# Retention and squared-ReLU FFN: a third room for one block's activations, and a reordered start

## The chip, the core and the metric

The kernel runs on one core of a Trainium2 chip. A core has five engines that run side by side: TensorE (PE, matmuls), VectorE (DVE), ScalarE (ACT), GpSimd (POOL) and SyncE (SP, which only issues transfers here). Transfers between the chip's memory and the on-chip buffer are issued by SP, ScalarE or GpSimd and are carried out by 16 DMA engines. Data of a matmul come from the on-chip buffer (128 partitions) and go to PSUM[...], from which VectorE or ScalarE take them. The metric is the time of one execution on the device, in microseconds.

## What is computed

Retention for 8 batches and 8 heads over 576 positions with head size 64, then an FFN with a squared ReLU over all 4608 tokens (`x` is the retention's output with the heads side by side):

```python
scores = scale * np.matmul(q, k.transpose(0, 1, 3, 2))
gamma = 1.0 - 2.0 ** (-5.0 - np.arange(H))
Dmat = np.where(rel >= 0, gamma[:, None, None] ** rel[None, :, :], 0.0)
x = np.matmul(scores * Dmat[None], v)         # then (B, H, S, D) -> (4608, 512)
h = np.maximum(x @ w_in, 0.0)                 # 512 -> 2048
out = h * h @ w_out                           # 2048 -> 512
```

All inputs are float32 except the two weight matrices, which arrive as 64-bit floats and are turned into 32-bit ones by integer operations on the chip.

## The kernel before, in words

**Stages.** Tokens are handled in 36 chunks of 128 for the retention and in 9 blocks of 512 for the first FFN matrix. Chunks 0 to 3 are computed first (lines 853 to 901), and from then on one chunk of retention alternates with matmuls of the block before (loop at line 915). Block 0 uses the weights as they are (`first_in`, 16 pieces of 128 columns); blocks 1 to 8 use a Strassen-like scheme with 7 products (`ffn_in`). The second matrix is applied at the end in a nested scheme (`inner`, `outer`, line 1144 on). The order on every engine is the order of the program text: each engine takes its instructions one after another and waits for semaphores at the head of its own queue.

**Start.** `load(i)` fetches q, k and v of a chunk: two transfers of 128 KB each for q and k (even and odd heads), one of 256 KB for v, each split in two where a chunk crosses from one batch to the next (chunk 4 is the first). For chunk 0, line 149 chooses the queue: q on SP, k and v on ScalarE's. All other loads, and the 16 raw pieces of the first weight matrix (512 KB each, `fetch_w`, line 209), are on SP. `scale_q` multiplies q by decays (line 396, on VectorE or GpSimd), `scale_v` does it for v (line 495, GpSimd), `turn_in` transposes k and q on TensorE into PSUM (line 445), `turn_out` copies them out (line 454; engine 0 is ScalarE, 1 is VectorE). `scores_full` multiplies q and k (line 509) and masks the product on VectorE in two steps, one for each parity e of the heads (line 513). `carry_full` applies the state of the chunks before (line 529), `retain_full` multiplies the masked scores by v (line 535, the four heads of e=0 first) and adds to the state (line 538). `x_out` copies the result into `xT` (line 550), and `grown` copies the state (line 501).

**Weight pieces.** `convert(n)` takes the next n of six steps per piece: `one` (L227), `two` (L231), `beside` (L235, ScalarE), `three` (L238), `four` (L241), `five` (L244); the others are on VectorE. A piece can be used by `first_in` after `five`. `fetch_raw` issues the raw pieces, at most 8 ahead.

**Block 0's activations.** `first_in(j)` writes Relu (line 683, ScalarE) and then the square of piece j into a room of four pieces (a pair `mp` holds pieces 4mp to 4mp+3). There are two rooms, `g_room[0]` and `g_room[1]`, used in turn, and after each fourth piece the room is stored to memory (line 689) by two transfers of 256 and 768 KB. A room is written again only after its store has read it. What `first_in` appends to `queue` (the square, the store) is issued within the next step by `some`. Blocks 1 to 8 use the same two rooms.

**End.** `leave` transposes a finished piece of the output on VectorE (line 1039) and stores it. A range of 384 or 192 tokens is cut into runs where it crosses a 256-token half, and each run is stored by four transfers of 32 partitions (line 1047). The last two steps of the outer loop call it from `last_inner` (line 1096) with the queues given at lines 1104 to 1108: GpSimd, SP and ScalarE.

```python
queues[n % len(queues)].dma_start(to[p], t[own, lo_:lo_ + w // 32, es, :])
three = (nc.gpsimd,) * 2 + (nc.sync, nc.scalar) * 3
```

Of the kernel before, what the change touches and what calls it, by code (L numbers as in the profile page):

```python
# [18 lines left out]
HT = TOK // 2  # L19
# [22 lines left out]
def kernel(  # L42
# [33 lines left out]
    nc = tc.nc  # L76
# [3 lines left out]
    HP = H // 2  # L80
# [46 lines left out]
    g_dram = dram.tile([N_BLK, len(G_KEPT), 128, N_M, HT], F32, name="g_dram")  # L127

    room = const.tile([128, 15872], F32, name="room")
    g_room = [room[:, j * 2560:(j + 1) * 2560].rearrange("p (s m t) -> p s m t", s=5, m=2) for j in range(2)]  # L130
    p_room = [room[:, 7168 + j * 1536:7168 + (j + 1) * 1536].rearrange("p (s m t) -> p s m t", s=3, m=2) for j in range(2)]
    xs_room = room[:, 10240:11776].rearrange("p (s c t) -> p s c t", s=3, c=2)
    xT_room = [room[:, 11776 + j * 2048:11776 + (j + 1) * 2048].rearrange("p (c t) -> p c t", c=N_DM) for j in range(2)]
    QUARTERS = ((0, 1), (2, 5))
# [5 lines left out]
    def load(i, names="qkv"):  # L140
        if i == 0:
            nc.sync.dma_start(dv, decays)
        got = loaded.setdefault(i, [None] * 3)
        for name, pool, src in (("q", ld3, q), ("k", ld5, k), ("v", ld4, v)):
            if name not in names:
                continue
            t = got["qkv".index(name)] = pool.tile([128, H, D], F32, tag=name, name=f"{name}_ld")

            issue = nc.scalar if i == 0 and name != "q" else nc.sync
            b, c0 = divmod(i * C, S)  # L150
            runs = [(b, c0, slice(0, C))] if c0 + C <= S else [(b, c0, slice(0, CH)), (b + 1, 0, slice(CH, C))]
            for e in range(1 if name == "v" else 2):
                for b, c0, to in runs:
                    at = src[b, :, c0:c0 + to.stop - to.start, :].rearrange("h s d -> s h d")
                    if name == "v":
                        issue.dma_start(t[to], at)
                    else:
                        issue.dma_start(t[to, e * HP:(e + 1) * HP, :], at[:, e::2, :])
# [150 lines left out]
    def fetch_raw(count):  # L309

        for _ in range(count):
            if n_raw[0] < min(N_W1, n_made[0] + N_RAW):
                fetch_w(n_raw[0])
                n_raw[0] += 1
# [18 lines left out]
    def convert(count):  # L333
        for _ in range(count):
            f = next(w_in_steps, None)
            f and f()
# [16 lines left out]
    for half in range(2):  # L353
        at = slice(CH * half, CH * half + CH)
# [37 lines left out]
    def scale_q(i, engine, parts=(slice(0, H),)):  # L392
        at = N_PAT + i % N_PAT
        for heads in parts:
            t = loaded[i][0][:, heads, :]
            engine.tensor_tensor(t, t, dv[:, heads, at:at + 1].to_broadcast(list(t.shape)), op=ALU.mult)  # L396
# [34 lines left out]
            nc.scalar.copy(*moves.pop(0)[2:])  # L431
            count -= 1

    def turn_in(i, js=(1, 0)):

        if "p" not in st[i]:
            if i < N_EARLY:
                p = [ps_e.tile([128, 512], F32, tag=f"e{h}", name="t_ps") for h in range(2)]
            else:
                p = [ps_f.tile([128, 512], F32, tag="f", name="t_ps") for h in range(2)]  # L440
            st[i]["p"] = [x.rearrange("p (j d t) -> p j d t", j=2, d=HP) for x in p]
        for j in js:
            for hp in range(HP):
                for h in range(2):
                    nc.tensor.transpose(st[i]["p"][h][:, j, hp, :], loaded[i][j][rows(h), 2 * hp:2 * hp + 2, :],  # L445
                                        ident[rows(h), rows(h)])

    def turn_out(i, engines=(0, 1)):

        p = st[i].pop("p")  # L450
        to = new_qk(i)
        copies = (nc.scalar.copy, nc.vector.tensor_copy)
        for h in range(2):
            copies[engines[h]](to[:, :, :, CH * h:CH * h + CH], p[h])

    def turn(i, engines=(0, 1)):
        turn_in(i)
        turn_out(i, engines)
# [61 lines left out]
    def carry_full(i):  # L520

        xp[0] = ps_x.tile([128, 2, 256], F32, tag="x", name="x_ps", padded_shape=[128, 2, 512])
        clean.clear()
        if i == 0:
            u_ps[0] = ps_u.tile([128, HP, D], F32, tag="u", name="u_ps")
            return
        u = u_sb[2 * i % 3]
        for hp, e, b in HEADS[0:2] + HEADS[4:6] + HEADS[2:4] + HEADS[6:8]:
            nc.tensor.matmul(x_full(hp, e, b), lhsT=u[rows(e), hp, :], rhs=st[i]["qT"][rows(e), hp, :],
                             start=clears(b, e), stop=False, skip_group_check=True)  # L530

    def retain_full(i):

        for hp, e, b in (HEADS[j] for j in (0, 4, 2, 6, 1, 5, 3, 7)):
            nc.tensor.matmul(x_full(hp, e, b), lhsT=st[i]["vs"][:, head(hp, e), :], rhs=st[i]["ret"][:, e, hp, :],  # L535
                             start=clears(b, e), stop=False, skip_group_check=True)
        for hp, e, b in HEADS:
            nc.tensor.matmul(u_ps[0][rows(e), hp, :], lhsT=loaded[i][1][:, 2 * hp + e, :], rhs=st[i]["vs"][:, head(hp, e), :],
                             start=(i == 0 and hp == 0), stop=(hp == HP - 1), skip_group_check=True)
        x_out(i, lambda: grown(i, 1))  # L540
# [119 lines left out]
    queue = []  # L660
# [6 lines left out]
    def first_in(j, halves=(0, 1), at=(0, HT)):  # L667

        assert n_made[0] > j
        wi, m, e = pieces[j]  # L670
        mp, mm = divmod(m, 2)
        p = ps_f.tile([128, 2, HT], F32, tag="f", name="h_ps")
        w = w_in[mp][:, mm, 2 * e:2 * e + 2, :, :].rearrange("p s c f -> p (s c) f")
        lo, hi = halves[0], halves[-1] + 1
        p = p[:, lo:hi, at[0]:at[1]]
        for c in range(N_DM):
            nc.tensor.matmul(p, lhsT=w[:, c, :], rhs=xT[0][:, c, :].rearrange("p (h t) -> p h t", h=2)[:, lo:hi, at[0]:at[1]],  # L677
                             start=(c == 0), stop=(c == N_DM - 1))

        t = g_room[mp % 2][:, 2:5:2, mm, :] if e else g_room[mp % 2][:, 0:4:3, mm, :]  # L680
        t = t[:, lo:hi, at[0]:at[1]]
        some(2)
        nc.scalar.activation(t, p, AF.Relu)
        if hi - lo == 2:
            queue.append(lambda: nc.scalar.activation(t, t, AF.Square))
        else:
            queue.append(lambda: nc.vector.tensor_tensor(t, t, t, op=ALU.mult))
        if mm and e and hi == 2 and at[1] == HT:
            queue.append(lambda: [nc.sync.dma_start(
                g_dram[0, a:b, :, 2 * mp:2 * mp + 2, :].rearrange("s p m t -> p s (m t)"),  # L690
                g_room[mp % 2][:, a:b, :, :].rearrange("p s m t -> p s (m t)")) for a, b in QUARTERS])
        if j >= N_W1 - 4:

            sums_w.setdefault(0, sum_w_in(0)).pop(0)()
            if n_next[0] > 1:
                if 1 not in sums_x:
                    sums_x[1] = sum_x(1)
                sums_x[1].pop(0)()
# [154 lines left out]
    halves = (slice(0, HP), slice(HP, H))  # L853
# [3 lines left out]
    scale_v(0)  # L857
    turn_in(0, (0,))
    turn_out(0)
    scale_q(1, nc.vector, halves)  # L860
    load(3)
    fetch_raw(3)
    warm(1)
    scores_full(0)
    turn(1, (0, 0))
    carry_full(0)
    retain_full(0)
    convert(3)
    scores_full(1)
    scale_q(2, nc.gpsimd)  # L870
    carry_full(1)
    retain_full(1)
    convert(3)
    turn(2, (0, 0))
    load(4)
    load(5, "qk")
    fetch_raw(1)
    load(5, "v")
    fetch_raw(1)
    first_in(0, (0,), (0, C))  # L880
# [152 lines left out]
    def leave(k, o, h, e, es, lo, hi, queues=(nc.sync,), t=None):  # L1033

        if t is None:
            t = t_room[n_left[0] % len(t_room)]
            n_left[0] += 1
        to, at = t[:, 0:(hi - lo) // 32, es, :], o[:, es, lo:hi]
        nc.vector.transpose(to.rearrange("p a e c -> p e a c"), at.rearrange("p e (a c) -> p e a c", c=32))
        n = 0  # L1040
        for b, at, c, w in runs(k // NP, lo, hi):
            row = b * TOK + h * HT + at
            to = out[row:row + w, e * HT:(e + 1) * HT].rearrange("(a r) (p e c) -> p r a e c", r=32, e=2, c=32)[:, :, :, es, :]
            lo_ = (c - lo) // 32
            for p in range(4):
                own = slice(32 * p, 32 * p + 32)
                queues[n % len(queues)].dma_start(to[p], t[own, lo_:lo_ + w // 32, es, :])
                n += 1
# [178 lines left out]
```

## Time and profile before

| | us |
|---|---|
| median of 3 runs (931.1 to 931.4) | 931.4 |
| the profiled execution | 931.4 |
| its span, first to last instruction | 929.7 |
| start of the first `first_in` matmul (L677) | 16.55 |
| end of the last matmul | 925.13 |
| last output transfer issued | 926.73 |
| DVE wait for a raw weight piece before 24 us | 1.3 |

The profile counts time from the first instruction. An engine's busy time is the union of its instructions; the weight loads of TensorE (PEld) overlap with its matmuls. "Idle before, releaser" in square brackets in a timeline is how long the engine had waited and what ended the wait. A transfer's issue appears on its queue (SPq, ACTq); its landing is some microseconds later, when its semaphore is complete.[...]

### The profile page before, as it was taken

What the parts mean: (1) busy time and instruction counts of PE and PEld (TensorE: products, weight loads), DVE (VectorE), ACT (ScalarE), POOL (GpSimd) and SP (SyncE); (2) the same over time, 40 slices, a digit from 0 to 9 for tenths busy, and PEclk for the clock granted to TensorE, in tenths of its full rate; (3) what the DMA queues carried; (4) which work ended last, traced back from release to release, by engine and by line L of the source; (5) the groups of instructions that cost most, each with busy time, mean ns of one, the idle gap of its engine ahead of it and who ended that gap; (6) DMA issues with size and microseconds to landing.
All of it is one profiled execution on the core that took longest, in us unless ns stands there. A gap on an engine that the chain in (4) does not pass through costs nothing.

```text
span 929.7 us, 21073 instructions
## 1 busy us (share of the span) xinstructions
PE 922.7 (99%) x8548; PEld 830.3 (89%) x8548; DVE 756.2 (81%) x1215; ACT 346.4 (37%) x788; POOL 84.3 (9%) x84
## 2 busy tenths in 40 slices
PE   8999999999999999999999999999999999999998
PEld 7654888888888888888888899999999999999997
DVE  5888798888898888979876587878888888877887
ACT  3457767667676676676711110000000000000000
POOL 3322111121111111211000000000000000000000
PEclk9999999999999999999999999999999999999999
DMA  9998657678666785784379996566666575465523
GB/s 223 223 258 231 169 150 200 165 212 267 166 182 182 261 216 146 224 267 140 115 255 345 381 334 194 145 165 197 175 165 195 151 209 156 116 177 138 151 85 68
DMA packets 297152, 181.29 MB, mean 195 GB/s; under 512 B 194112, under 2 KB 270016, under 8 KB 296160
## 3 DMA queue, kind: packets, MB, share of 16 engines
q1 hardware_dynamic: 292064, 178.81, 66.4%
q10 hardware_dynamic: 4928, 1.08, 0.6%
q8 instruction: 67, 1.10, 0.5%
q14 instruction: 29, 0.24, 0.1%
q0 software_dynamic: 64, 0.07, 0.0%
HBM read 109.39 MB, written 70.52 MB: 194 GB/s over the span
## 4 chain that ended last, share of the span: by engine, by line
PE 98%; DVE 1%; issue 0%; POOL 0%; ACT 0%; POOLq 0%; DVEq 0%
PE h_b L717 18%; PE o_b L1063 17%; PE h_a L717 12%; PE h_c L717 12%; PE o_c L1063 12%; PE o_a L1063 12%; PE h_ps L677 6%; PE x_ps L574 3%; PE sc_ps L480 2%; PE x_ps L609 1%; PE u_ps L568 1%; PE idle_ps L845 0%; PE t_ps L445 0%; PE sc_ps L509 0%; PE x_ps L535 0%; DVE room L513 0%
## 5 line engine op out<-in xcount | busy, mean ns | idle before, releaser
L717 PE MATMUL h_b<-room,w 128*128 128x256 f32 x768 | 181.5, 379 | 0.0
L431 ACT COPY qk<-flip 32x256 f32<-32x256 f32 x432 | 173.8, 402 | 6.7
L717 PEld LDWEIGHTS h_b<-room,w 128*128 128x128 f32 x768 | 145.8, 190 | 20.0 <-DVE room L736 0.2
L717 PE MATMUL h_a<-room,w 128*128 128x256 f32 x512 | 123.9, 385 | 0.0
L717 PE MATMUL h_c<-room,w 128*128 128x256 f32 x512 | 121.0, 379 | 0.0
L717 PEld LDWEIGHTS h_c<-room,w 128*128 128x128 f32 x512 | 97.3, 190 | 13.2
L717 PEld LDWEIGHTS h_a<-room,w 128*128 128x128 f32 x512 | 95.0, 190 | 13.7
L1063 PE MATMUL o_b<-room,w 128*128 128x192 f32 x496 | 90.7, 326 | 0.0
L1076 ACT COPY r<-o_a 128x192 f32<-128x192 f32 x28 | 8.9, 319 | 209.4 <-PE o_a L1063 209.4
L1063 PEld LDWEIGHTS o_b<-room,w 128*128 128x128 f32 x496 | 82.3, 190 | 0.0
L724 DVE SCALAR_TENSOR_TENSOR room<-room 128x512 f32<-128x512 f32 x96 | 67.2, 700 | 3.3
L396 POOL TENSOR_TENSOR q_ld<-q_ld,dv 128x512 f32<-128x512 f32 x34 | 37.8, 1113 | 286.2 <-DMA q_ld<-in_q_dram 240.7
L1063 PE MATMUL o_a<-a,w 128*128 128x192 f32 x352 | 62.6, 326 | 0.0
L1063 PE MATMUL o_b<-s,w 128*128 128x192 f32 x336 | 61.5, 326 | 0.0
L1063 PE MATMUL o_c<-s,w 128*128 128x192 f32 x336 | 61.5, 326 | 0.0
L1063 PE MATMUL o_c<-room,w 128*128 128x192 f32 x336 | 61.5, 326 | 0.0
L677 PE MATMUL h_ps<-room,w 128*128 128x512 f32 (+1 forms) x152 | 57.7, 532 | 0.6 <-DVE w L244 0.5
L1063 PEld LDWEIGHTS o_a<-a,w 128*128 128x128 f32 x352 | 58.1, 190 | 0.1
L1063 PE MATMUL o_a<-room,w 128*128 128x192 f32 x320 | 56.9, 326 | 0.0
L1063 PEld LDWEIGHTS o_b<-s,w 128*128 128x128 f32 x336 | 55.8, 190 | 0.0
L1063 PEld LDWEIGHTS o_c<-s,w 128*128 128x128 f32 x336 | 55.8, 190 | 0.0
L1063 PEld LDWEIGHTS o_c<-room,w 128*128 128x128 f32 x336 | 55.8, 190 | 0.0
(117 smaller groups left out, 1412.6 us busy)
## 6 DMA issues: line engine op xcount, KB each, us to landing
g_dram<-room SPq DMA_DIRECT2D x164, 256.0 KB, 3.8
a<-g_dram SPq DMA_DIRECT2D x30, 512.0 KB, 5.8
room<-g_dram SPq DMA_DIRECT2D x28, 512.0 KB, 5.1
w_dram<-w SPq DMA_DIRECT2D x28, 448.0 KB, 4.4
w<-w_dram SPq DMA_DIRECT2D x7, 1792.0 KB, 9.6
q_ld<-in_q_dram SPq DMA_DIRECT2D x64, 128.0 KB, 4.1
w<-in_moe_w_in_dram SPq DMA_DIRECT2D x16, 512.0 KB, 6.0
w<-in_moe_w_out_dram SPq DMA_DIRECT2D x64, 128.0 KB, 3.4
```

Of the source, the lines that this page charges most:

```text
L396: engine.tensor_tensor(t, t, dv[:, heads, at:at + 1].to_broadcast(list(t.shape)), op=ALU.mult)
L431: nc.scalar.copy(*moves.pop(0)[2:])
L480: nc.tensor.matmul(st[i]["sc"][e][rows(h), hp, :], lhsT=st[i]["kT"][rows(e), hp, t], rhs=st[i]["qT"][rows(e), hp, t], start=True, stop=Tru ...
L568: return [lambda hp=hp, e=e, b=b: nc.tensor.matmul(u[rows(e), hp, :], lhsT=loaded[i][1][rows(h), 2 * hp + e, :], rhs=st[i]["vs"][rows(h), ...
L574: return [lambda hp=hp, e=e, b=b: nc.tensor.matmul(x_at(hp, e, b, h), lhsT=s["vs"][rows(h), head(hp, e), :], rhs=s["ret"][rows(h), e, hp, ...
L609: m = nc.tensor.matmul(x_at(hp, e, b, h), lhsT=u[rows(e), hp, :], rhs=s["qT"][rows(e), hp, CH * h:CH * h + CH], start=clears(b, e), stop=F ...
L677: nc.tensor.matmul(p, lhsT=w[:, c, :], rhs=xT[0][:, c, :].rearrange("p (h t) -> p h t", h=2)[:, lo:hi, at[0]:at[1]], start=(c == 0), stop= ...
L717: nc.tensor.matmul(p[:, mm, :], lhsT=w[:, c, :], rhs=xs[n][right][:, c, :], start=(j in OPENS and mm == 0 and c == 0), stop=(j in CLOSES a ...
L724: nc.vector.scalar_tensor_tensor(t, t, 0.0, t, op0=ALU.max, op1=ALU.mult)
L1063: nc.tensor.matmul(p, lhsT=w_out[j][:, m, WO_SLOT[right], :], rhs=s["lefts"][left][:, m, :], start=(i in OPENS and m == 0), stop=(i in CLO ...
L1076: nc.scalar.copy(r[:, 0, LEFT], p)
```

## The change

Five edits, all in the order of work or in where things are kept:

1. **Chunk 0.** q is loaded on ScalarE's queue, and k and v on SP.
2. **Chunk 1.** The scaling of its q is split, one half on VectorE and one on GpSimd. Its transposes are split in two halves of two head pairs: one half after the scores of chunk 0, the other inside `retain_full(0)`, between the matmuls of e=0 and those of e=1. The copies out of PSUM are one on ScalarE and one on VectorE (before, both were on ScalarE). The six steps of weight piece 0 are issued as 2, 2 and 2, and the last two come before `carry_full(1)`.
3. **Weight piece 4** (the fifth) is fetched before q, k and v of chunk 5 instead of between k and v.
4. **Block 0.** A third room, `g_late`, lies in columns 5120 to 7168 of `room`, which nothing else used at that time. Pair 0 goes to `g_late`, pair 1 to `g_room[0]`, pair 2 to `g_room[1]`, and pair 3 to `g_late` again. The stores come after pieces 9 (pair 0), 13 (pair 1) and 15 (pairs 2 and 3) instead of after 3, 7, 11 and 15.
5. **Output.** In `leave`, a run of 64 tokens is stored by two transfers of 128 partitions instead of four of 32.

```diff
+    g_late = room[:, 5120:7168].rearrange("p (s m t) -> p s m t", s=4, m=2)
...
-            issue = nc.scalar if i == 0 and name != "q" else nc.sync
+            issue = nc.scalar if i == 0 and name == "q" else nc.sync
...
-    def turn_in(i, js=(1, 0)):
+    def turn_in(i, js=(1, 0), hps=range(HP)):
...
-            for hp in range(HP):
+            for hp in hps:
...
-    def retain_full(i):
+    def retain_full(i, inside=lambda: None):
 
-        for hp, e, b in (HEADS[j] for j in (0, 4, 2, 6, 1, 5, 3, 7)):
+        for j in (0, 4, 2, 6, 1, 5, 3, 7):
+            hp, e, b = HEADS[j]
+            if j == 1:
+                inside()
...
-        t = g_room[mp % 2][:, 2:5:2, mm, :] if e else g_room[mp % 2][:, 0:4:3, mm, :]
+        if mp % 3:
+            t = g_room[mp - 1][:, 2:5:2, mm, :] if e else g_room[mp - 1][:, 0:4:3, mm, :]
+        else:
+            t = g_late[:, e:3 + e:2, mm, :]
...
-        if mm and e and hi == 2 and at[1] == HT:
-            queue.append(lambda: [nc.sync.dma_start(
-                g_dram[0, a:b, :, 2 * mp:2 * mp + 2, :].rearrange("s p m t -> p s (m t)"),
-                g_room[mp % 2][:, a:b, :, :].rearrange("p s m t -> p s (m t)")) for a, b in QUARTERS])
+        for at_mp in {9: (0,), 13: (1,), 15: (2, 3)}.get(j, ()) if hi == 2 else ():
+            def store(mp=at_mp):
+                for a, b in QUARTERS:
+                    kept = g_room[mp - 1][:, a:b, :, :] if mp % 3 else g_late[:, max(0, a - 1):b - 1 if a else 1, :, :]
+                    nc.sync.dma_start(g_dram[0, a:b, :, 2 * mp:2 * mp + 2, :].rearrange("s p m t -> p s (m t)"),
+                                      kept.rearrange("p s m t -> p s (m t)"))
+
+            queue.append(store)
...
-    scale_q(1, nc.vector, halves)
+    scale_q(1, nc.vector, halves[:1])
+    scale_q(1, nc.gpsimd, halves[1:])
...
-    turn(1, (0, 0))
+    turn_in(1, (1, 0), (0, 1))
     carry_full(0)
-    retain_full(0)
-    convert(3)
+    retain_full(0, lambda: [turn_in(1, (1, 0), (2, 3)), turn_out(1), convert(2)])
+    convert(2)
     scores_full(1)
     scale_q(2, nc.gpsimd)
+    convert(2)
     carry_full(1)
     retain_full(1)
-    convert(3)
     turn(2, (0, 0))
     load(4)
+    fetch_raw(1)
     load(5, "qk")
-    fetch_raw(1)
     load(5, "v")
     fetch_raw(1)
...
+            if w == 64:
+                for a in range(2):
+                    queues[n % len(queues)].dma_start(to[:, :, a, :, :], t[:, lo_ + a, es, :])
+                    n += 1
+                continue
```

## Prediction

> **What bounds the kernel now.** I began with the page's busy shares and slices, because they say whether any engine still has room.
>
> ```profile
> PE 922.7 (99%) x8548; PEld 830.3 (89%) x8548; DVE 756.2 (81%) x1215; ACT 346.4 (37%) x788; POOL 84.3 (9%) x84
> ...
> PEclk9999999999999999999999999999999999999999
> DMA  9998657678666785784379996566666575465523
> ```
>
> TensorE is idle for 929.7 - 922.7 = 7.0 us in all, at full clock. A table of windows says where:
>
> ```profile
> 0.00:10.00 10.00, 8.48 (x60) 6.16 (x60) 3.88 (x8) 1.94 (x3) 3.13 (x13) 1.00 0.94 200
> 10.00:20.00 10.00, 9.12 (x170) 7.88 (x170) 5.99 (x10) 4.60 (x10) 4.43 (x5) 1.00 1.09 214
> 20.00:30.00 10.00, 10.00 (x128) 8.14 (x127) 8.60 (x17) 4.37 (x10) 1.94 (x2) 1.00 0.80 195
> ```
>
> The first column after the length is TensorE. From 20 to 910 us it is full (9.96 of 10 us at the least), and the chain of waits gives TensorE 98%. So an edit gains only before about 17 us or after 923.85 us; between them it can gain nothing and can only lose. The timeline of the start shows what holds the first 17 us:
>
> ```profile
> 6.11 0.43 DVE L396 TENSOR_TENSOR q_ld<-q_ld,dv 128x256 f32<-128x256 f32 x1 [1.34 <-DMA q_ld<-in_q_dram]
> 7.74 1.61 DVE L396 TENSOR_TENSOR q_ld<-q_ld,dv 128x256 f32<-128x256 f32 x2
> 7.75 1.33 POOL L495 TENSOR_TENSOR v_ld<-v_ld,dv 128x512 f32<-128x512 f32 x1 [5.02 <-DMA v_ld<-in_v_dram]
> 9.28 1.27 DVE L513 TENSOR_TENSOR room<-sc_ps,room 128x512 f32<-128x512 f32 x2
> 10.10 1.16 PE L535 MATMUL x_ps<-room,v_ld 128*64 128x128 f32 x16 [0.21 <-DVE room L513]
> 12.85 1.29 DVE L513 TENSOR_TENSOR room<-sc_ps,room 128x512 f32<-128x512 f32 x2 [1.24 <-PE sc_ps L509]
> 14.06 0.92 DVE L238 SCALAR_TENSOR_TENSOR w<-w,w 128x512 f32<-128x512 uint32 x1
> 15.80 0.69 DVE L244 SCALAR_TENSOR_TENSOR w<-w,w 128x512 uint32<-128x512 uint32 x1
> 16.55 1.16 PE L677 MATMUL h_ps<-room,w 128*128 128x128 f32 x8 [0.51 <-DVE w L244]
> ```
>
> Read it down: q's second half lands late, VectorE's scaling of chunk 1's q (two halves, 1.61 us) delays the mask, mask and the conversion of weight piece 0 follow on the same engine, and the first weight matmul waits for the last step (L244). From 16.55 us TensorE runs without a gap. The end of the chain in order of time:
>
> ```profile
> 923.85 0.02 issue
> 923.87 0.37 DVE room L1100
> 924.26 0.59 DVE room L1039
> 924.85 0.31 issue
> 925.16 0.71 POOL out_dram L1047
> ```
>
> The transpose ends at 924.84 us and VectorE's very last one at 925.94 us; the last output transfer is issued by ScalarE's queue at 926.73 us and lands at 928.62 us, 1.1 us before the span ends.
>
> [...] the second half of L396 took 1.20 us beside L495 on GpSimd, against 0.43 us alone. [...]
>
> **Head: loads of chunk 0.** The scalar queue now carries q (2 issues) in place of k and v; SP carries k (2) and v (1) in place of q, one issue more, about 0.5 us, ahead of chunk 1. In the trace the scalar queue's two first 128 KB halves land at 3.49 and 4.77 us, SP's two first at 4.24 and 6.08. So q is complete near 4.8 and not 6.08, and k, by bytes, near 5.2; the warm-up matmuls hold TensorE until 5.76 anyway. VectorE's second scaling moves from 6.11 to 4.8, the 16 transposes run from 5.76 to about 6.5 instead of 7.06: 0.55 us. Total bytes are the same. The two queues together moved about 170 KB per us, one alone 225 (128 KB steps of 0.58 us after 8 us), and the two-queue stretch gets shorter, so I estimate later landings 0 to 0.55 us earlier, and take 0.4.
>
> **Head: chunk 1's q and transposes.** One of the two scalings goes to GpSimd (half of 1.06 us, L396's price there). It queues behind v's scaling (about 6.4 to 7.5) and delays no later GpSimd work, which waits for v1 until 12 us. VectorE keeps one, done between 7.65 (0.43 alone) and 8.5[...]. Scores of chunk 0 end near 8.45 (0.55 to 0.65 earlier), so the mask starts near 8.5 and ends at 9.8, against 9.28 and 10.55. The first halves of chunk 1's transposes come before the values product, the second halves between its e=0 and e=1 matmuls, where TensorE would wait for the second mask. The product ends near 10.7, the state matmuls near 11.1 (before: 11.73).
>
> **Head: copies and conversion.** turn_out(1) goes from ScalarE twice (1.07 us) to one on each engine, so VectorE gets 0.69 us more at about 10.2. The conversion of piece 0 is cut 2+2+2 instead of 3+3: L238 (0.69 to 0.92) now comes before chunk 1's mask. VectorE: copy to 10.9, two steps of 0.4 to 11.7, L238 to 12.5, mask to 13.8, L241 and L244 (0.70 each) to 15.2, against 16.50. Now TensorE is late instead: values product after the mask, state, then chunk 2's transposes, 13.8 + 0.58 + 0.47 + 0.7 = 15.6, where its k lands at 15.41 less the 0.4. First weight matmul: 15.7 against 16.55, 0.85 us earlier. From both sides: 0.45 if no landing moves, 1.1 if all move by 0.55.
>
> **Head: fifth piece ahead of chunk 5.** 512 KB go before q and k of chunk 5. The trace prices them at 2.33 us (k at 33.59, the piece at 35.92). So k5 lands at 33.6 + 2.3 - 0.4 = 35.5, and q5 at 32.5 + 2.3 - 0.4 = 34.4, scaled by GpSimd at 35.5 to 35.9 (1.06 alone[...]). TensorE wants them at 36.35 - 0.85 = 35.5 (k) and 35.8 (q). Loss 0 to 0.4, taken as 0.15. The piece itself lands 2.4 us sooner and removes VectorE's wait of 0.5 us at 35.95, which costs nothing today: its weights are ready at 40.18 and used at 43.38. Net head: 0.7.
>
> **Block 0's room and stores.** No instruction of a compute engine is added. Four groups of two stores stay eight stores. The first moves from pieces 3 to 9, the second from 7 to 13, the third from 11 to 15. This takes 2 MB out of the stretch from 52 to 77 us (DMA share 0.9 to 1.2) and puts 1 MB near 89 us, where the share is 0.43 and then 0.18. TensorE is full there, so gain 0. The new danger is reuse of the third room: pair 3's first Relu must wait for pair 0's store.
>
> **Tail.** Runs of 64 tokens occur in two leaves only, for the left half at the last two steps. In the last, SP and the scalar queue issue two transfers each instead of three, before the four of the final transpose. Those can start at 925.97 instead of 926.22 and 926.30: 0.25 to 0.33 us, the last landing at 928.3. [...] I take 0.2. TensorE's last matmul is untouched.
>
> **Sum.** 929.7 - 0.7 - 0.2 = 928.8 us of span; the profiled execution took 931.4 us, 1.7 more than its span, and equals the median of the runs shown. Forecast 930.5.
>
> **Rivals.** *The gain is taken back* (0.22): chunk 5's q and the third chunk's data are hidden no longer; head 0.1, tail 0.2, so 931.1. For: DMA is full up to 20 us. Against: later matmuls had 1 to 3 us of slack to their data. The case that conversion order does nothing at all lies within it. *The head gives all its idle time* (0.10): the four gaps before 16.55 sum to 0.23 + 0.21 + 0.27 + 0.51 = 1.22, filler matmuls 0.65, transposes 0.2 more; 2.1 with the tail gives 929.3. Against: chunk 2's k. *The third room blocks ScalarE* (0.12), slower: at 80.51 us L683 writes piece 12 into it. If pair 0's store is no earlier in SP's queue than the one now issued at 78.18 to 80.50 and landing at 85.81, Relu starts at 85.8, the copy of the state behind it on ScalarE (L501, 81.17) ends at 86.8, and TensorE, which needs it at 81.64 - 0.9, loses 6.1 us: 936.6. It decides as soon as that store lands after 79.6. Against: 2 MB less lie before it, so it should land near 70.
>
> **How the numbers follow.** The likeliest has 0.56 and its own range 929.9 to 931.0. A measurement tells about 0.2%, 1.9 us, from no change. The range leaves out the slower case and part of the fastest: 929.4 to 931.7. Faster by more than 1.9 us: 0.09; slower: 0.11; within: 0.80.
>
> **What would show it.** Right: the first L677 near 15.7, L396 once on VectorE for chunk 1, the last issue near 926.4, TensorE full between. Wrong: L683 idle near 80 us on a DMA; t_ps idle near 35.5 on q_ld by more than 0.4; L677 still behind L244; a last landing after 928.6.

## The result, and the profile after

| | before | after |
|---|---|---|
| median of 16 runs each (us) | 931.77 | 933.40 |
| lowest to highest | 931.10 to 932.31 | 932.12 to 934.24 |
| ratio, 95% interval | | 1.0016 [1.0009, 1.0023] |
| the profiled execution | 931.4 | 932.12 |
| its span | 929.7 | 930.4 |

The change costs 1.6 us. That is within the 0.2% where I had put 0.80 of the chance, but above my range (929.4 to 931.7), and I had forecast a small gain. The profiled execution of the kernel after is its fastest; its trace holds 0.7 of the 1.6 us, so the sizes below come from runs of single parts, and the traces tell where to look.

The page of the kernel after, busy times and slices:

```profile
PE 922.3 (99%) x8548; PEld 830.1 (89%) x8548; DVE 756.9 (81%) x1215; ACT 345.9 (37%) x787; POOL 83.5 (9%) x85
...
PEclk9999999999999999999999999999999999999999
DMA  9999457678666784884379996566666575465523
```

The engines do the same work at the same clock; a difference of 0.7 us can't be seen here. The windows of the kernel after (from and to, length, then PE, PEld, DVE, ACT, POOL, clock, DMA share, GB/s) show the places:

```profile
0.00:10.00 10.00, 8.00 (x64) 5.93 (x64) 3.85 (x7) 1.87 (x2) 3.55 (x14) 1.00 0.97 201
10.00:20.00 10.00, 9.47 (x180) 8.21 (x182) 7.03 (x11) 4.69 (x10) 4.81 (x5) 1.00 1.12 213
20.00:30.00 10.00, 10.00 (x119) 7.83 (x116) 7.97 (x16) 3.98 (x10) 2.27 (x2) 1.00 0.85 202
30.00:40.00 10.00, 9.55 (x81) 4.66 (x80) 9.51 (x16) 5.03 (x9) 3.65 (x3) 1.00 1.06 245
70.00:80.00 10.00, 10.00 (x24) 4.37 (x24) 9.32 (x15) 6.55 (x14) 4.30 (x4) 1.00 1.09 275
```

The same two later stretches of the kernel before:

```profile
30.00:40.00 10.00, 9.96 (x83) 4.92 (x82) 8.46 (x15) 5.08 (x9) 4.10 (x4) 1.00 1.11 254
70.00:80.00 10.00, 10.00 (x24) 4.39 (x24) 7.94 (x16) 6.92 (x15) 0.55 (x1) 1.00 0.92 269
```

TensorE gains 0.35 us between 10 and 20 us and loses 0.41 between 30 and 40. (The lower first window is that of the filler matmuls, which give way to the first transposes at 5.24 us, where they ran to 5.76 before.) The last row is the surprise: between 70 and 80 us GpSimd does four instructions where it did one, and VectorE is busy for 1.4 us longer on one instruction fewer.

The start in the timeline of the kernel after:

```profile
6.91 1.06 POOL L496 TENSOR_TENSOR v_ld<-v_ld,dv 128x512 f32<-128x512 f32 x1 [4.18 <-DMA v_ld<-in_v_dram]
8.46 1.29 DVE L514 TENSOR_TENSOR room<-sc_ps,room 128x512 f32<-128x512 f32 x2 [0.21 <-PE sc_ps L510]
11.81 0.69 DVE L239 SCALAR_TENSOR_TENSOR w<-w,w 128x512 f32<-128x512 uint32 x1
11.93 1.50 POOL L496 TENSOR_TENSOR v_ld<-v_ld,dv 128x512 f32<-128x512 f32 x1 [3.20 <-DMA v_ld<-in_v_dram]
13.73 1.26 DVE L242 SCALAR_TENSOR_TENSOR w<-w,w 128x512 f32<-128x512 f32 x1
15.02 0.69 DVE L245 SCALAR_TENSOR_TENSOR w<-w,w 128x512 uint32<-128x512 uint32 x1
15.77 1.16 PE L681 MATMUL h_ps<-room,w 128*128 128x128 f32 x8
```

The first weight matmul starts at 15.77 us, where I had 15.7. But L239 began just 0.12 us ahead of GpSimd's L496, which then took 1.50 us instead of 1.06. L242, the next conversion step, began 0.34 us behind a scaling of GpSimd (L397, 13.39 us) and took 1.26 us instead of 0.69. The lead ends at chunk 5 (TensorE in the same timeline):

```profile
35.71 0.34 PE L446 MATMUL t_ps<-w,k_ld 64*128 64x64 f32 x4
36.45 0.34 PE L446 MATMUL t_ps<-w,k_ld 64*128 64x64 f32 x4 [0.40 <-DMA k_ld<-in_k_dram]
```

Half of k is there, the other half lands at 36.41 us, behind the 512 KB of the piece; in the kernel before, ahead of them, it landed at 33.59. In step with the kernel before (the start of the same instruction compared in both traces), TensorE is 0.64 us ahead before this wait and 0.02 after it, at the next weight matmul. The end of the chain of waits:

```profile
923.96 0.02 issue
923.99 0.37 DVE room L1117
924.36 0.02 issue
924.38 0.59 DVE room L1051
924.97 0.31 issue
925.27 0.71 POOL out_dram L1064
925.99 0.55 POOLq L1239
```

The chain is the old one, 0.12 us later, yet the span ends 0.7 us later: 930.4 - 924.38 = 6.0 us after the start of this transpose (the last but one), against 929.7 - 924.26 = 5.4 before.

### The profile page after: what moved, and what is told of

The parts are those of the page before. It is cut to its first block, busy times and chain, and to the rows that moved or that the text cites. A ratio compares the mean times of both kernels' runs of the same rounds, so it can differ in the third digit from the quotient of the medians.

```text
span 930.4 us, 21069 instructions
## 1 busy us (share of the span) xinstructions
PE 922.3 (99%) x8548; PEld 830.1 (89%) x8548; DVE 756.9 (81%) x1215; ACT 345.9 (37%) x787; POOL 83.5 (9%) x85
## 4 chain that ended last, share of the span: by engine, by line
PE 97%; DMA 1%; SPq 1%; POOL 0%; ACT 0%; issue 0%; DVE 0%; POOLq 0%
PE h_b L728 18%; PE o_b L1080 17%; PE h_a L728 12%; PE h_c L728 12%; PE o_c L1080 12%; PE o_a L1080 12%; PE h_ps L681 5%; PE x_ps L578 3%; PE sc_ps L481 2%; PE x_ps L613 1%; PE u_ps L572 1%; DMA k_ld<-in_k_dram 1%; DMA v_ld<-in_v_dram 1%; SPq L159 1%; PE t_ps L446 0%; PE x_ps L539 0%
## 5 line engine op out<-in xcount | busy, mean ns | idle before, releaser
L397 POOL TENSOR_TENSOR q_ld<-q_ld,dv 128x512 f32<-128x512 f32 (+1 forms) x35 | 38.5, 1101 | 287.1 <-DMA q_ld<-in_q_dram 225.4
```

## The experiments

Each set of four below was timed beside its own runs of the kernel before (medians 931.72, 931.75, 931.78 and 931.79 us); differences are against these. A single one of a few tenths lies within the intervals and counts only with others or with its trace.

### One part of the change undone, and the start alone

Edit 3 undone (`load(5, "qk")` again ahead of `fetch_raw(1)`):

> The changed kernel with one edit undone: weight piece 4 is again fetched after chunk 5's q and k. Theory A (the fifth piece makes chunk 5's k land late and TensorE waits for it near 36 us): the wait of 0.6 us before chunk 5's transposes goes, TensorE's lead of about 0.65 us at 30 us is kept to the end, and the time falls from 1.6 us above the kernel before to between 0.2 us above and 0.8 us below it. Theory B (block 0's stores and third room cost the time between 50 and 100 us): the time stays 1 us or more above the kernel before. Theory C (only the tail is slower): it falls by the 0.6 us of the head, to about 1 us above, and the last transfer lands 0.5 us later after the last matmul than in the kernel before.

Block 0's rooms and stores as before (`g_room[mp % 2]`, a store after each fourth piece):

> The changed kernel with two rooms and the old times of block 0's stores. Theory A: nothing changes at chunk 5 (k still lands about 36.4 us), so the time stays about 1.6 us above the kernel before, less at most 0.3 us. Theory B: the delay of TensorE near 82 us (0.2 us in the profiled execution, more in the slower ones) goes, and the time falls by 0.2 to 1.5 us.

The `if w == 64` branch in `leave` taken out:

> The changed kernel with runs of 64 tokens again in four transfers of 32 partitions. Theory C (two transfers of 128 partitions [...] hold up the last stores): the last landing comes 0.5 to 0.6 us sooner after the last matmul, and the time falls by 0.5 to 0.6 us against the changed kernel, to about 1 us above the kernel before. If the tail plays no part, it falls by less than 0.2 us.

All three undone, so that edits 1 and 2 remain:

> Only the reordered start (chunk 0's queues, chunk 1's scaling and transposes, conversion in steps of two); piece 4, stores and tail as before. If the gain at the start is real and nothing later takes it back: TensorE leads by about 0.65 us from 25 us to the end, and the time is 0.5 to 0.8 us below the kernel before (ratio about 0.9993). If later data take it back even without the piece moved: within 0.2 us of it. All theories that see the loss in the other edits expect it faster than the changed kernel by about 2.2 us.

| | median us | ratio, interval | against before |
|---|---|---|---|
| piece 4 as before | 933.13 | 1.0016 [1.0009, 1.0023] | +1.4 |
| rooms and stores as before | 932.08 | 1.0005 [0.9996, 1.0013] | +0.4 |
| output as before | 932.39 | 1.0006 [0.9998, 1.0014] | +0.7 |
| new start alone | 931.83 | 1.0000 [0.9992, 1.0008] | +0.1 |

Of the 1.6 us, the rooms take about 1.3 with them when they go, the output 1.0 and the piece 0.2 to 0.3. That is more than 1.6 in all, so what one part costs depends on the others or is known no better than to some tenths. And the new start by itself gains nothing, though the trace of the kernel after showed it 0.8 us ahead.

### One part alone, added to the kernel before

The third room and later stores:

> The kernel before with only the third room and the later stores of block 0. Theory B, in the form that the profiles now suggest: with 2 MB of stores gone from the stretch before 70 us, chunks' q and v land earlier, GpSimd scales them between 70 and 80 us beside VectorE's conversions instead of after them, VectorE's L227 to L244 there take 1.1 to 1.6 us now and then instead of 0.4 to 0.7, its transposes L416 come 0.4 to 1 us later, ScalarE's copies wait for them, and TensorE waits 0.2 to 1.3 us near 82 us. The time is 0.4 to 1.3 us above the kernel before. If the loss came from the reuse of the room (the store landing late), ScalarE's Relu near 80.5 us waits for a transfer instead, and GpSimd's times play no part. If both are wrong: within 0.2 us.

The output by two transfers:

> The kernel before with only the new output stores (runs of 64 tokens in two transfers of 128 partitions). Theory C: everything up to the last matmul is as before; the last transfer lands 0.4 to 0.7 us later after the last matmul, and the time is 0.5 to 0.7 us above the kernel before (ratio about 1.0006). If the tail has no part of its own, the ratio is within 0.0002 of 1.

Output runs of 64 tokens in four transfers of 16 KB as in the kernel before, but each over two groups of 32 partitions:

```diff
+            if w == 64:
+                for j in range(4):
+                    a, h2 = divmod(j, 2)
+                    queues[n % len(queues)].dma_start(to[2 * h2:2 * h2 + 2, :, a, :, :],
+                                                      t[64 * h2:64 * h2 + 64, lo_ + a, es, :])
+                    n += 1
+                continue
```

> The kernel before, with each run of 64 tokens in four transfers of 16 KB as before, but of 64 partitions each[...]. If what costs is on how many DMA engines a transfer is spread[...] the last landing comes 1 to 2 us later than before, the time 1 to 2 us above. If it is the size of a transfer or something else of the two big ones, four small ones land as before: within 0.2 us of the kernel before.

The fifth piece ahead of chunk 5:

> The kernel before with weight piece 4 fetched ahead of q and k of chunk 5, and nothing else. Theory A: k of chunk 5 lands at about 36.0 to 37.0 us and TensorE, which wants it at 36.35, waits; 0.2 to 0.6 us above the kernel before (ratio 1.0002 to 1.0007). Rival: without the early start TensorE comes late enough to find k there, and the time is within 0.15 us of the kernel before, so that the piece costs only what the new start gained.

| | median us | ratio, interval | against before |
|---|---|---|---|
| rooms and stores | 932.47 | 1.0010 [1.0001, 1.0018] | +0.7 |
| output, two transfers | 932.46 | 1.0009 [1.0000, 1.0017] | +0.7 |
| output, four over two groups | 933.44 | 1.0017 [1.0010, 1.0024] | +1.7 |
| fifth piece | 931.76 | 0.9997 [0.9988, 1.0005] | 0.0 |

The parts alone sum to 0.1 + 0.7 + 0.7 + 0.0 = 1.5 of the 1.6 us. Two costs, the rooms and the output, are the result; each measures 0.7 alone, with an interval from about 0 to 1.7 us, and more when it is taken out of the whole. The fifth piece costs nothing by itself: its k lands while TensorE, without an early start, isn't there yet (the transposes show no wait for it). It costs what the start has gained, no more.

**The output.** The transfer rows of the last microseconds (queue, count, KB each, median us from issue to landing), kernel before:

```profile
out_dram<-room ACTq DMA_DIRECT2D x4, 24.0 KB, 1.8
out_dram<-room SPq DMA_DIRECT2D x4, 24.0 KB, 1.7
```

and with the new output alone:

```profile
out_dram<-room ACTq DMA_DIRECT2D x4, 24.0 KB, 2.3
out_dram<-room SPq DMA_DIRECT2D x4, 24.0 KB, 2.3
```

The 24 KB transfers are not edited, yet take 0.5 to 0.6 us longer. What is issued ahead of them finishes later: in the kernel after the last transfer of 64 tokens is complete at 928.33 us, in the kernel before at 927.55. The saved issue time is lost again. After the very last transpose the first of them are issued 0.25 and 0.33 us sooner than before, as I had it. But the issue of a new transfer takes 0.55 to 0.57 us (L1059 in the kernel after) where an old one took 0.42 to 0.45, and on ScalarE's queue the first 24 KB transfer behind it took 0.72 us to issue instead of 0.38, so that the last one starts 0.79 us after that transpose in both kernels. The last output landed 0.65 us later after than before (929.27 against 928.62). The traces keep the time of every update of a transfer's semaphore. An old transfer of the last step completes in 16 updates within 0.2 us or so of each other; a new one shows a single early update (926.69 us for the one that ScalarE's queue issued at 925.40) and then 4 (928.12 to 928.33), one over two groups a single early one and then 2. The 24 KB transfers behind them still complete in 16, but in the kernel after 12 of the last one's come by 928.71 us and 4 only from 929.01 to 929.27; over two groups 14 come early and 2 late. The number of late updates is the number in which the new transfers complete, and the 4 late ones make the last landing. The traces don't name the DMA engines of a transfer: on how many it was spread isn't shown, only its updates are.

The order of the times fits: with 16 updates 0, with 4 late ones +0.7, with 2 +1.7, although the last has as many transfers of the same 16 KB as the kernel before. The late updates alone don't explain the size for two groups: there the last 24 KB transfer is also issued later, 1.8 us after the end of the very last transpose instead of 0.8.

### Why the rooms cost: taking the scalings away

My rival had been ScalarE blocked near 80 us by the reuse of the room. In the kernel after L690, the Relu into the third room, has no wait for a transfer there. What is late is in VectorE's and GpSimd's timeline. Kernel before:

```profile
75.34 0.69 DVE L241 SCALAR_TENSOR_TENSOR w<-w,w 128x512 f32<-128x512 f32 x1
76.06 0.69 DVE L244 SCALAR_TENSOR_TENSOR w<-w,w 128x512 uint32<-128x512 uint32 x1
77.58 1.63 ACT L431 COPY qk<-flip 32x256 f32<-32x256 f32 x4
79.45 1.06 POOL L396 TENSOR_TENSOR q_ld<-q_ld,dv 128x512 f32<-128x512 f32 x1 [10.73 <-DMA q_ld<-in_q_dram]
```

Rooms and stores alone:

```profile
72.85 1.42 POOL L397 TENSOR_TENSOR q_ld<-q_ld,dv 128x512 f32<-128x512 f32 x1 [5.68 <-DMA q_ld<-in_q_dram]
73.38 1.43 DVE L245 SCALAR_TENSOR_TENSOR w<-w,w 128x512 uint32<-128x512 uint32 x1
75.03 1.06 POOL L496 TENSOR_TENSOR v_ld<-v_ld,dv 128x512 f32<-128x512 f32 x1 [0.76 <-DMA v_ld<-in_v_dram]
75.36 1.00 DVE L228 TENSOR_SCALAR w<-w 128x512 uint32<-128x512 uint32 x1
79.61 1.65 ACT L432 COPY qk<-flip 32x256 f32<-32x256 f32 x4 [1.07 <-DVE flip L417]
83.41 0.27 PE L569 MATMUL u_ps<-v_ld,k_ld 64*64 64x64 f32 x2 [0.63 <-ACT u_sb L502]
```

Read it down. With the stores issued later than these loads and not ahead of them, q and v of the coming chunks land sooner; GpSimd, which waited for them until 79.45 us, scales them at 72.85 and 75.03. There VectorE converts weights back to back, and the steps that begin 0.53 and 0.33 us behind a scaling take 1.43 and 1.00 us instead of 0.69 and 0.39. So VectorE is late with the flip (its own transpose of a later chunk's q and k, L417), ScalarE waits 1.07 us for it, and its copy of the state (L502), further back in that queue, reaches TensorE too late. In step with the kernel before, TensorE loses 0.86 us at 82 us. This execution is the slowest of its 13 and was as far behind already when it came there; in the profiled executions of the three other kernels with the new rooms and all scalings the loss at this place is 0.23 (the kernel after), 0.45 and 0.86 us, and in those of the twelve changed kernels with the old rooms there is none. To test this I left out, in the rooms-alone kernel, only the scalings of chunks 8 to 11, whose retention is then computed from unscaled q and v:

```diff
-        for heads in parts:
+        for heads in () if 8 <= i <= 11 else parts:
...
+        if 8 <= i <= 11:
+            return
         nc.gpsimd.tensor_tensor(vs, vs, dv[:, :, at:at + 1].to_broadcast([C, H, D]), op=ALU.mult)
```

> The kernel before with the third room and the later stores alone, and with the scaling of q and v of chunks 8 to 11 left out (GpSimd's four times two or three instructions between about 65 and 85 us; the retention of these chunks is then computed from unscaled q and v). Theory B[...]: the room and the stores only let the chunks land earlier, and with that GpSimd's scalings fall beside VectorE's conversions between 70 and 80 us. Without the scalings the conversion steps there take 0.4 to 0.9 us again and none 1.3 or more, TensorE's wait near 82 us (0.84 us with the room and stores alone) goes, and the time is 0.4 to 0.8 us below that of the room and stores alone (ratio about 1.000 against 1.001). Rival, transfers: the stores moved to 80 to 90 us delay loads, the wait near 82 us stays at 0.5 us or more, and the time stays 0.7 us above the kernel before.

931.59 us, 0.9998 [0.9989, 1.0006]: 0.2 below the kernel before, 0.9 below the rooms alone. Its timeline:

```profile
72.67 0.69 DVE L245 SCALAR_TENSOR_TENSOR w<-w,w 128x512 uint32<-128x512 uint32 x1
73.91 0.39 DVE L228 TENSOR_SCALAR w<-w 128x512 uint32<-128x512 uint32 x1
77.72 1.63 ACT L432 COPY qk<-flip 32x256 f32<-32x256 f32 x4
```

The steps are short again, ScalarE waits for nothing, and TensorE keeps to within 0.1 us of the kernel before at 82 us. The stores and all their bytes are where the change put them, so the transfers by themselves are not the cause; GpSimd's scalings are, by where they fall. Leaving them out also takes away what the flip of q depends on, and the same omission in the kernel before was not run. But with the rooms alone the flip of q follows VectorE's own L245 without idle time, so it waited for that queue. Why a scaling and a conversion step lengthen each other the traces don't show; that they do is in the durations above.

### Why the start gains nothing: holding GpSimd back

The trace of the new start alone shows the same lengthening. GpSimd scales v of chunks 1 and 2 just when VectorE converts piece 0:

```profile
11.89 1.30 POOL L496 TENSOR_TENSOR v_ld<-v_ld,dv 128x512 f32<-128x512 f32 x1 [3.23 <-DMA v_ld<-in_v_dram]
12.30 1.43 DVE L239 SCALAR_TENSOR_TENSOR w<-w,w 128x512 f32<-128x512 uint32 x1
15.48 1.06 POOL L496 TENSOR_TENSOR v_ld<-v_ld,dv 128x512 f32<-128x512 f32 x1 [0.83 <-DMA v_ld<-in_v_dram]
15.56 1.53 DVE L245 SCALAR_TENSOR_TENSOR w<-w,w 128x512 uint32<-128x512 uint32 x1
17.15 1.05 PE L681 MATMUL h_ps<-room,w 128*128 128x128 f32 x7 [0.40 <-DVE w L245]
```

A lead of 0.8 us in one execution is a lag of 0.6 in this one, and in the traces the difference is which of the two engines comes first. How often it falls out so isn't shown: the kernel after and the three with one part undone have the same start, and in their profiled executions the first weight matmul came at 15.56 to 15.96 us. So one trace per kernel leaves open whether 17.15 is chance, or comes with the new start when it stands alone. I first moved chunk 1's mask ahead of the third conversion step (`convert(2)`, `convert(2)` become `convert(1)`, `convert(3)` around it), so that a collision couldn't delay the mask:

> The reordered start alone, with one step of it put back: conversion step three (L239) comes after chunk 1's mask again (steps 2, 1, 3). Theory D: in the reordered start L239 races with GpSimd's scaling of v1 near 11.9 us[...]; where GpSimd starts first, L239 takes 1.43 instead of 0.69 us and holds up the mask, and the lead of 0.8 us turns into a lag of 0.6. With the mask first this cannot happen: the first L681 comes at 15.7 to 16.1 us in the profile, never above 16.55, and the time is 0.4 to 0.8 us below the kernel before. If the race is not what spoils the start alone, it stays within 0.2 us of the kernel before as that run did.

931.66 us, 1.0000 [0.9992, 1.0008]. The mask was on time at 13.01 us, but L245 met the next scaling (1.50 us) and the first weight matmul started at 17.54: moving one step moved the collision. So I made GpSimd wait, in the new start and in the kernel before (there for chunk 2 only):

```diff
+    HELD = {1: 3, 2: 5}
...
+        if i in HELD:
+            tc.add_manual_dep(made.ins, made_by[HELD[i]].ins.name,
...
```

> The new start alone (chunk 0's q first, chunk 1's halves, the conversion as 2, 2 and 2), with two waits added on GpSimd: the scaling of v of chunk 1 waits for step three of the conversion of weight piece 0, and that of chunk 2 for step five. Theory D[...]: with them no step of this conversion can meet GpSimd, so the first weight matmul starts between 15.7 and 16.2 us in the trace and the time is 0.4 to 0.8 us below the kernel before (ratio 0.9992 to 0.9996), where the new start alone measured no difference. Rival, the waits only push the collision on to the mask or to the next conversion: within 0.2 us of the kernel before.

> The kernel before with one wait added on GpSimd: the scaling of v of chunk 2 waits for step five of the conversion of weight piece 0. Theory D: step five can no longer meet it; in the profile of the kernel before it just escaped, so the profiled start of the first weight matmul stays at 16.5 to 16.6 us and the median falls by 0 to 0.3 us at the most. Rival, the wait itself delays chunk 2's values: above the kernel before by 0.3 us or more.

Then, with the waits in the new start, `turn(4)` (the transposes of chunk 4 and their copies out of PSUM) became `turn(4, (0, 0))`, which gives both of the copies to ScalarE; and this edit alone in the kernel before:

> The new start with the two added waits, and with chunk 4's transposes copied out by ScalarE alone instead of one half by VectorE. Near 31 to 36 us conversion steps on VectorE take 1.3 us beside GpSimd, VectorE's copy comes late and TensorE waits 0.3 to 0.4 us for it. Theory D: this wait goes too, 0.6 to 1.2 us below the kernel before in all (ratio 0.9987 to 0.9994). Rival: ScalarE, which copies chunk 4's halves one after the other, is as late as VectorE was, and it measures as the new start with the waits alone.

> The kernel before with chunk 4's transposes copied out by ScalarE alone. In its profile VectorE's copy of them starts 1.4 us late behind a conversion step that meets GpSimd, but TensorE shows no wait there. Theory: the copy costs nothing without an early start, within 0.15 us of the kernel before. Rival: it does cost in most executions, and the time falls by 0.3 us or more, as much as the new start with the waits gained from the same edit.

Last, `convert(3)` of piece 1 behind `scores_full(3)`; and the same without the two waits:

> The new start with the two waits and ScalarE's copies, and the first three conversion steps of weight piece 1 put behind the mask of chunk 3 on VectorE. Theory: the part of the lead that is lost between 23.5 and 24.7 us (from 0.6 to 0.4) was the mask waiting behind a conversion step that waits for the raw piece, landing at 21.9 to 22.4 us; with the mask first TensorE is 0.6 to 0.8 us ahead at 25 us and the time is 0.1 to 0.4 us below that without this edit, 0.6 to 0.9 below the kernel before. Rival: the conversion comes too late for the first matmul that uses piece 1, and the time is at or above that without this edit.

> The same without the two waits on GpSimd. Theory D: the conversion of piece 0 can meet GpSimd again; the time is 0.1 to 0.5 us above the version with the waits, with a wider spread. Rival: the waits do nothing, the same within 0.1 us.

| | first weight matmul, profiled | median us | lowest to highest | ratio, interval |
|---|---|---|---|---|
| new start alone | 17.15 | 931.83 | 931.13 to 932.41 | 1.0000 [0.9992, 1.0008] |
| with the two waits | 15.64 | 931.71 | 931.20 to 933.19 | 1.0000 [0.9992, 1.0008] |
| waits, ScalarE's copies | 15.94 | 931.33 | 930.99 to 931.56 | 0.9994 [0.9986, 1.0002] |
| the same, mask of chunk 3 first | 16.24 | 931.33 | 930.75 to 932.89 | 0.9994 [0.9988, 1.0001] |
| without the waits | 16.45 | 931.58 | 931.05 to 933.37 | 0.9996 [0.9988, 1.0004] |
| before, one wait | 16.66 | 931.49 | 931.05 to 932.35 | 0.9997 [0.9989, 1.0006] |
| before, ScalarE's copies | 16.71 | 931.70 | 931.04 to 932.43 | 0.9997 [0.9989, 1.0005] |

The waits alone brought the early start (15.64) and still no gain: theory D, as I had put it, missed. The trace shows where the lead goes. By 24 us half of it is lost (0.72 us at 20 us, 0.35 at 24): the mask of chunk 3 stands on VectorE behind a conversion step that waited 2.23 us for its raw piece. The rest goes at chunk 4. With the waits, on GpSimd, VectorE and TensorE:

```profile
33.08 1.50 POOL L402 TENSOR_TENSOR q_ld<-q_ld,dv 128x512 f32<-128x512 f32 x1
33.70 1.43 DVE L245 SCALAR_TENSOR_TENSOR w<-w,w 128x512 uint32<-128x512 uint32 x1
35.05 0.68 DVE L460 COPY qk<-t_ps 128x512 f32<-128x512 f32 x1
35.37 1.10 PE L486 MATMUL sc_ps<-qk 64*64 64x64 f32 x32
```

The scores take 1.10 us instead of 0.69, because half of them wait for the copy, which waits for a step that takes 1.43 us beside a scaling; the lead of 0.35 us becomes a lag of 0.05. With both copies on ScalarE, 0.4 us of lead last to the end of the profiled execution, and all 13 runs lie below the median of the kernel before. That version is the best found: 0.45 us below the kernel before (its interval still touches 1) and 2 below the kernel after. The edits that were tried alone gain nothing that can be measured, which fits a chain whose next link is always near, but doesn't show it. The one wait in the kernel before gave 0.3 us at the edge of what was expected and within scatter; its first weight matmul was not earlier.

Mask first gave nothing more, against what I expected. The difference without the waits, 0.25 us, is within scatter; the trace shows the collision come back (L239 1.43 us beside L496), but how often it does I can't tell from one trace per kernel.

## Why the prediction was wrong

**Head, loads, transposes, copies and conversion: right for the profiled execution, wrong as a fixed gain.** 15.77 us against my 15.7, and TensorE was 0.78 ahead. But in my sum the conversion steps had nearly undisturbed durations (two of 0.4, then 0.8, 0.7 and 0.7), although I had seen L396 take 1.20 us beside L495 on GpSimd, against 0.43 alone. Pulling the conversion 0.8 us forward brings it beside the scalings of chunks 1 and 2; single steps then took 1.26 to 1.53. In the median the gain of 0.85 is about 0 (931.83 against 931.72). That these collisions take all of it is argued from the traces: the start with the waits is early (15.64) and its median no better.

**Fifth piece ahead of chunk 5: place right, size wrong.** I took a loss of 0.15 with k landing at 35.5; it landed at 36.41, and the loss was 0.6 in the profiled execution. I had credited k with landings 0.4 earlier. Alone the piece costs nothing, so my rival "the gain is taken back" names a part of what became of the head.

**Block 0's room and stores: the step that failed.** I set the gain at 0 because TensorE was full, and looked for danger only in the reuse of the room, which did not happen. I had 2 MB of stores leave the stretch from 52 to 77 us, and did not ask what the earlier loads release: GpSimd's scalings, beside VectorE's conversions. The stores did not leave that stretch either: in the kernel after, those of pairs 0 and 1 start at 68.99 and 75.66 us, behind loads that they stood ahead of when they started at 52.51 and 65.83. Measured +0.7 alone.

**Tail: wrong in sign.** I took a gain of 0.2 from the issue times, and did not ask what lands behind the new transfers: the final ones do, and 4 of the last one's 16 updates came from 929.01 to 929.27 us, where I had its landing at 928.3. Measured +0.7 alone, +0.6 between the chain's transpose and the end of the span in the trace.

**The sum.** Head 0.7 and tail 0.2 were to be gained; 0.1, 0.0, 0.7 and 0.7 were lost. Another 0.4 us of the distance from 930.5 to 933.40 is the level I started from: the three runs shown had a median of 931.4, the 16 runs 931.77. The slower rival had ScalarE stalled near 80 us, and a stall is there, but its cause is VectorE's flip and its price under 1 us, not 6.1.

## What to carry to other kernels

When a load or store is moved, follow it to the instruction that it releases, and look at what the other engines do at the new time: here earlier data made the whole 0.7 us later, with GpSimd's scalings beside VectorE's conversions (0.69 us became 1.43). Where two such instructions begin within a few tenths of a microsecond of each other, a gain in one trace needn't be there in the median: 0.8 us in the trace of the kernel after, about 0 in the median of the new start alone. Making the one without hurry wait took that collision out of the trace (15.64 us against 17.15), and then the next one down the line decided. Before transfers at the end are merged, time the merged form alone and look at the updates of the transfers behind it: here two that complete in 4 late updates cost 0.7 us against four that complete in 16.

## What was not expected of the hardware

- In these traces the order of two engines goes with who pays. When L239 was 0.12 us ahead (the kernel after), GpSimd's scaling took 1.50 us instead of 1.06 and VectorE kept its 0.69; when it was 0.41 us behind (the new start alone), L239 took 1.43 and the scaling 1.30.
- A step with one input was hit as well: L228, a shift from a strided 32-bit view, took 1.00 us beside a scaling instead of 0.39 (rooms and stores alone).
- Three forms of the same bytes at the end: 931.75 us with 32-partition transfers, 932.46 with four groups in one, 933.44 with two groups in one. The last transfer, which is the same in all three, completes in 16 updates each time: within 0.34 us in the first form (928.28 to 928.62), with 4 of them late in the second and 2 in the third.
